# A fused window-attention and expert kernel: first loads as half rows on one queue, mask products on GpSimd only, and a new instruction order

## The chip, the cores and the metric

The kernel runs on one core of a Trainium2 chip. The core has a matrix engine (TensorE), a vector engine (VectorE, DVE in the profile), an activation engine (ScalarE, ACT), a general engine (GpSimd, POOL) and a queue engine (SyncE, SP) that here only issues transfers. The engines run side by side and wait for each other on semaphores. Matmul results go to PSUM, which here is four tiles of two banks. The metric is the time of one execution on the device in microseconds; lower is better. The median of three runs decides.

## The reference

The input is q, k and v of shape (8 batches, 8 heads, 576 tokens, 64). A sliding-window attention comes first, and its output, heads side by side, is the input x of a mixture of four attention experts:

```python
scores = scale * np.matmul(q, k.transpose(0, 1, 3, 2))
mask = np.abs(pos[:, None] - pos[None, :]) <= 32
attn = softmax(np.where(mask, scores, -1e9))          # over keys
x = (attn @ v).transpose(0, 2, 1, 3).reshape(8, 576, 512)

logits = x @ w_gate                                   # 4 experts, the best 2 are kept
w = softmax(the two largest logits)
for e in range(4):
    a = softmax(causal(scale * (x @ wq[e]) @ (x @ wk[e]).T))
    out += (e is chosen) * w[e] * (a @ (x @ wv[e]) @ wo[e])
```

Everything is float32 outside. Inside, the window attention and the gate are in float32, the experts in bfloat16.

## The kernel before

The program is a straight list of steps, written out by hand as text in `ORDER` (895 steps). A loop at the end of the kernel calls one small function for each word. Each engine executes its own instructions in the order of that list, so a step that waits holds up all later steps of the same engine. The letters of a word name the function; the digits name batch, head group (heads 0 to 3 or 4 to 7), half of the tokens, pair of heads or part; after the `@` come the PSUM banks, and the engine of the step where there is a choice (a for ScalarE, v for VectorE, g for GpSimd). The steps of one batch b are:

- `lq`, `lk`, `lv`: load q, k (one head group: 576 KB) and v (128 tokens of all heads: 256 KB). `load` makes each of them wait until the last matmul that stands before it in the list is done. They are all issued by SyncE.
- `tq`, `tk` (`turn`): q and k come with 18 consecutive tokens in one partition, a head in 32 partitions. VectorE transposes 32 x 32 blocks into `QKT`, one transpose for each half of the head dimension.
- `sc`: scores of one head group and one half of the queries, 80 matmuls on 32 rows each, only on the key blocks that the window touches.
- `ex`: ScalarE takes the exponential into `A` (`AT`); there are three such buffers, one for each head group in flight.
- `mk`: `A` times the 0/1 window mask `MASKP`, two heads and 288 queries at once (128 x 576 float32). Eight of these for each batch, 64 in all. `s_mask` builds `MASKP`.
- `vc`: shifted copies of v inside SBUF.
- `av`, `un`: attention times v for 128 tokens, with the row sum as a 65th column, and the division on VectorE into `XN`. The parts T = 0 and 1 (queries 32 to 287) need the four masked products of the first half, T = 2 and 3 (288 to 543) those of the second half, and T = 4 (the first and the last 32 queries) all eight.
- `xt`, `xf`, `xb`: transposes of x on TensorE (with `ident`, built by `s_ident`), copy to `XTF` in float32, cast to `XTB` in bfloat16.
- `ga`, `gt`, `ge`, `gm`, `gu`: the gate. `pp`, `pe`, `pv`, `ve`: expert projections and their evictions. `ps`, `xe`, `se`: expert scores, exponential, causal mask on GpSimd. `po`, `oe`, `ox`, `py`, `ye`, `st`: the values, weights, output projection and store.
- `wl`, `cw`: weight loads and casts. `s_...`: constants and fills. `s_wm`: 30 matmuls on zeros at the start. `s_pada` fills part of the three `ATE` buffers.

Batch 0 starts differently. `fq`, `fk` (`first_load`) and `gq`, `gk` (`first_turn`) load and turn its q and k. For head group 0 the tokens come in two parts of consecutive tokens (tokens 0 to 287 and 288 to 575 for q, 0 to 319 and 320 to 575 for k), one transfer for each head: 16 transfers of 64 to 80 KB. The k transfers are issued by SyncE, the q transfers by ScalarE. Head group 1 comes in one transfer of 576 KB each.

All but one of the 64 mask products run on GpSimd; the step `mk0001@v` puts one of batch 0 on VectorE. Around it, the list reads

```
mk0110@g vc01@g lv12 wl0 ex0100@4 ex0101@0 sc100@62 av03@0 vc00@a wl1 ex1001@2 ex1000@6 mk0101@g tq11
mk0001@v av02@4 sc101@62 mk0100@g tk11 un03@0 un02@4 cw0@a ex1010@6 lq20 mk1001 mk1000 mk1010 ex1011@2
av01@0 un01@0 ...
```

All engine instructions pass through one helper, so nearly all have its line, L145, in the profile; they are told apart by the names of the tiles. Loads are L234 (`load`), L366 and L370 (`first_load`).

Of the kernel before, what the change touches and what calls it, by code (L numbers as in the profile page):

```python
# [20 lines left out]
HS = 288  # L21
# [3 lines left out]
    s_ident s_mask s_padv@g s_onev fq01 s_onep fk00 fk01 fq10 gk00 s_warm fq00 gq01 gk01 gq10 fk10 s_wm lv02  # L25
    lk10 sc001@02 lv00 lv01 lq10 gq00 sc000@46 ex0011@2 ex0010@0 gk10 ex0000@4 tk10 lv03 lq11 sc011@02 lv04
    lk11 ex0110@0 sc010@40 mk0011@g ex0111@2 s_pada@g mk0000@g mk0010@g mk0111@g ex0001@6 tq10 s_padx
    mk0110@g vc01@g lv12 wl0 ex0100@4 ex0101@0 sc100@62 av03@0 vc00@a wl1 ex1001@2 ex1000@6 mk0101@g tq11
    mk0001@v av02@4 sc101@62 mk0100@g tk11 un03@0 un02@4 cw0@a ex1010@6 lq20 mk1001 mk1000 mk1010 ex1011@2
    av01@0 un01@0 lk21 av00@4 lk20 un00@4 xt01@2 av04@0 xf01@2a cw1@a xt00@4 un04@0 xf00@4v xb00@v xb01@g  # L30
    xt02@0 sc110@26 xf02@0a xb02@g mk1011 lv11 lv14 ex1100@2 ex1101@6 tq20 sc111@04 ex1111@4 pp001@2
    pe001@2a lv13 mk1101 pp000@4 ex1110@0 pe000@4a lv10 pp011@6 tk20 pe011@6a wl2 pp010@0 ps000@6 ps003@4
    tk21 ga0@2 gt0@2 gm0@2 pe010@0a xe003@4 xe000@6 mk1111 mk1110 mk1100 ge0@2 gu0@2 vc11@g sc201@40
    ex2010@4 lq21 ps002@6 av14@3 xe002@6 ex2011@0 av13@4 lv23 un14@3 ps011@6 ps001@2 un13@4 mk2010 se001
    vc10@g av12@0 cw2@v xe011@6 lv33 xe001@2 lq30 un12@0 sc200@46 ex2001@6 xt12@2 xf12@2a xt11@0 ex2000@4
    tq21 mk2001 ps013@6 xf11@0a xe013@6 av10@2 un10@2 lv20 lv21 av11@4 ps012@6 xb11@g xe012@6 sc211@20
    ex2111@0 ex2110@2 lv22 wl3 un11@4 xt10@4 sc210@06 tq30 xb12@v ps010@2 xf10@4a lk31 ex2100@0 xe010@2
    ex2101@6 xb10@v se003 mk2000 ga1@4 lq31 pp101@0 pp100@6 lv24 lv30 gt1@4 gm1@4 ge1@4 mk2011 gu1@4
    pe101@0v pv10@2 pp110@0 lv32 vc21@a lk30 mk2100 se011 se000 mk2101 ve10@2a cw3@a pv00@4 pe100@6v
    pe110@0a ps100@2 ps102@0 mk2110 mk2111 av24@6 ve00@4a tk31 pv01@7 av23@4 xe100@2 tq31 un24@6 av22@2 lv31  # L40
    xe102@0 pv11@6 vc31@a lk40 ve11@6a ve01@7a un23@4 un22@2 vc20@g se010 av21@0 av20@4 sc311@62 ex3111@2
    mk3111 se013 un21@0 lq41 ps103@0 un20@4 xt21@4 lq40 xe103@0 ex3110@6 po000@2 pp111@6 xf21@4a xb21@g
    vc30@g tk30 oe000@2 pe111@6a po010@4 ps110@6 lv44 lv34 oe010@4 sc300@20 xt22@4 xf22@4v xb22@g xe110@6
    ex3001@0 ex3000@2 xt20@6 xf20@6v xb20@v ps111@4 sc301@20 ox00 xe111@4 tq40 tk40 ex3011@0 ex3010@2 ox01
    lv42 lv40 sc310@64 ps112@0 se103 mk3000 ex3101@4 mk3101 xe112@0 se111 mk3110 pv20@2 lv43 ve20@2a
    ex3100@6 mk3100 mk3010 py01@0 py00@4 ye00@4a ye01@0v mk3001 lk41 pp200@2 pe200@2v tq41 pp201@6 pe201@6a
    sc401@40 lq50 sc400@62 ex4010@4 lq51 ex4011@0 ex4000@6 ex4001@2 ga2@4 ps113@6 mk3011 xe113@6 ps101@0
    tk41 ps200@2 pv21@5 xe101@0 se110 se113 vc41@g mk4001 mk4000 mk4010 av30@6 lv41 gt2@4 xe200@2 un30@6
    av32@0 un32@0 ve21@5a lk51 se101 av31@2 py02@5 un31@2 av33@6 ps201@0 ps203@2 ye02@5a ge2@4 st02 xe203@2
    gm2@4 un33@6 mk4011 av34@5 lk50 xt30@2 xe201@0 lv54 gu2@4 un34@5 xf30@2a po110@6 pp210@0 pe210@0a  # L50
    sc411@24 ex4110@2 ex4111@4 oe110@6 se100 sc410@06 ex4101@6 ex4100@0 tq50 xt31@2 xt32@4 st01 ox11 po100@6
    tk50 xf32@4a xf31@2a pp211@4 xb30@g pe211@4a mk4111 oe100@6 sc500@20 ex5001@0 ex5000@2 sc501@46 ga3@0
    ox10 st00 ex5011@6 ex5010@4 lv50 lv52 ps212@6 tq51 xb32@v ps202@2 ps213@4 mk4100 mk4110 se200 xb31@v
    mk4101 xe213@4 av44@1 mk5001 mk5011 vc40@g mk5000 xe202@2 pp300@4 xe212@6 gt3@0 ge3@0 gm3@0 un44@1
    pe300@4v gu3@0 pp301@2 pe301@2a lv51 lq60 pp311@6 tk51 pe311@6a mk5010 vc50@g ps210@2 xe210@2 ps211@0
    ps300@4 xe300@4 av40@6 av41@2 av43@4 un40@6 xe211@0 ps301@0 xe301@0 ps303@6 se203 se201 se211 se213
    xe303@6 un41@2 lv53 un43@4 av42@2 un42@2 lq61 pv31@4 py12@5 sc511@60 ye12@5a ve31@4a lk60 ex5110@6
    ex5111@0 sc510@42 ex5100@4 ex5101@2 xt40@6 tq60 lv63 xf40@6v se210 mk5111 xt42@0 pp310@4 pe310@4a py10@2
    ye10@2a st10 po210@6 xt41@4 xf41@4a xf42@0a pv30@2 tk60 oe210@6 ve30@2a lv61 xb41@v mk5100 se303 mk5101
    se300 po200@4 ps312@6 xe312@6 oe200@4 ps310@0 xb40@g xe310@0 xb42@g lv62 ox20 st12 lv60 ox21 ga4@2 lq71  # L60
    ps313@6 ps302@4 xe313@6 xe302@4 mk5110 av54@3 sc601@60 ex6011@0 gt4@2 ge4@2 gm4@2 tq61 pp401@4 pe401@4v
    un54@3 gu4@2 ex6010@6 pp400@0 pe400@0a pv40@6 xt52@3 ve40@6a xf52@3v py11@0 ye11@0v ps403@2 xe403@2 lk61
    ps311@4 ps402@6 xe311@4 xe402@6 vc51@g se313 se311 se301 se310 se401 av51@2 un51@2 pv41@0 py22@1 av52@4
    ye22@1v lk70 ve41@0v vc60@a un52@4 av53@6 av50@0 ps401@4 lk71 xe401@4 un53@6 ps400@2 un50@0 xt51@6
    xf51@6a xt50@0 xf50@0a xb50@g xb51@g mk6010 mk6011 lv71 tk61 xb52@v pp411@4 po300@6 xe400@2 pe411@4a
    oe300@6 po310@0 oe310@0 sc610@42 ex6101@2 ex6100@4 pp410@6 pe410@6a ox31 sc600@20 lq70 ex6001@0 sc611@64
    ex6110@6 ex6000@2 ex6111@4 lv73 se400 se403 pp500@0 pp501@6 pe500@0a tk70 pe501@6v tq71 lv64 lv72 py21@2
    mk6101 py20@0 ye21@2a ps500@6 ps501@4 ye20@0a mk6100 vc61@g mk6001 mk6111 mk6000 lv74 ox30 st20 pv50@2
    pp510@0 xe500@6 xe501@4 tq70 pe510@0v ve50@2a pp511@4 mk6110 vc71@g ps410@2 lv70 pe511@4a ps412@0
    ps411@6 xe410@2 av60@4 av61@2 xe412@0 xe411@6 un60@4 pv51@0 py32@1 vc70@g un61@2 st11 ve51@0a ye32@1a  # L70
    av63@4 ps503@2 xe503@2 un63@4 ps502@6 xe502@6 po400@0 ps510@4 oe400@0 xe510@4 ps511@6 xe511@6 av62@2
    sc700@04 ga5@6 ex7000@0 ex7001@4 ps413@0 un62@2 xe413@0 se413 se503 se411 tk71 ps512@2 ps513@4 ox40
    av64@7 xt60@0 xe512@2 xe513@4 xt61@4 gt5@6 ge5@6 xf60@0a un64@7 xt62@7 se410 po410@2 gm5@6 py31@0
    xf61@4a xf62@7v xb60@v oe410@2 ye31@0v mk7000 xb62@g ga6@7 sc711@24 ex7110@2 ex7111@4 xb61@g se510
    pp600@0 gt6@7 ge6@7 pp601@2 pe601@2a pe600@0a gu5@6 gm6@7 gu6@7 pp610@4 pe610@4a sc710@26 se501 mk7110
    mk7111 se513 ex7100@2 se500 ex7101@6 sc701@40 ex7010@4 ex7011@0 pp611@2 pe611@2a py30@4 mk7001 ps600@0
    ps601@2 ye30@4v se511 xe601@2 po500@6 xe600@0 st21 ox41 py40@4 ye40@4a mk7100 mk7101 mk7010 oe500@6 st32
    st22 st31 se600 po510@2 oe510@2 ps613@6 xe613@6 ps611@0 ps612@4 av71@6 ox50 un71@6 st40 ox51 xe611@0
    xe612@4 mk7011 py42@2 av70@0 ye42@2v st42 av73@4 pv61@2 un70@0 ve61@2a av72@6 st30 un73@4 un72@6 ps603@2
    ps602@0 ps610@4 se613 xe603@2 av74@2 se611 xe602@0 xe610@4 xt70@6 py51@0 xt71@4 un74@2 xt72@2 xf70@6a  # L80
    xf71@4a xb70@v xf72@2a xb71@v xb72@g pv60@6 py50@2 ve60@6a se601 se610 ye50@2a pp700@4 py41@6 pe700@4v
    ye41@6v se603 pp711@2 po610@4 pp701@6 ye51@0a pe701@6a pp710@0 pe711@2v pe710@0a po600@2 ps713@0 xe713@0
    se713 oe610@4 st50 oe600@2 ps710@6 xe710@6 ps711@4 xe711@4 st41 ga7@0 ps712@6 xe712@6 gt7@0 ge7@0 gm7@0
    gu7@0 ps700@2 pv70@4 ps703@6 xe700@2 se711 ps701@2 xe703@6 py52@0 pv71@1 ps702@6 xe701@2 se710 ve70@4v
    ve71@1v ye52@0v se700 se703 ox61 po711@4 oe711@4 st51 xe702@6 ox60 py60@2 po701@0 oe701@0 po712@6
    oe712@6 se701 po702@4 pt711@0 st52 oe702@4 ye60@2a ot711@0a py61@2 pt701@0 ye61@2a ot701@0v py62@1
    pt712@4 ot712@4v pt702@5 st60 st61 ot702@5a ye62@1a py70@6 st62 ye70@6a st70 py72@0 ye72@0a st72 py71@4
    ye71@4a st71
"""


class Watched:

    def __init__(self, tc):
# [52 lines left out]
def kernel(  # L149
# [12 lines left out]
    nc = Watched(tc)  # L162
# [195 lines left out]

    FIRST = {"qn": ((0, 9), (9, 18)), "kn": ((0, 10), (10, 18))}

    def first_load(nm, src, q_, g, x):
        t = NAT[nm][g][:, :, :].rearrange("p o d -> p (o d)")
# [16 lines left out]
    def fk(g, x):  # L381
        first_load("kn", k, nc.sync, g, x)
# [329 lines left out]
```

The softmax here doesn't subtract the row's maximum and nothing guards it: scores larger than these inputs give would overflow.

## Time and profile before

| what | before |
|---|---|
| time, median of 3 runs | 245.62 us (244.63 to 248.32) |
| span of the profiled execution | 242.5 us |
| VectorE product A, MASKP | 1 in 7.34 us |
| GpSimd products A, MASKP | 63, mean 1428 ns |
| VectorE transposes of q and k, 128 x 576 | 60, mean 1240 ns |
| transfers | 42.94 MB, mean 177 GB/s |

The span is the time from the first to the last instruction of one profiled execution. The busy time of an engine is an average over the whole span; what an edit is worth is seen only in its own stretch of the timeline. The start of the kernel, in which loads, transposes, scores and masks of the first batches must follow each other, differs from the rest, in which batches overlap. GpSimd's idle time before its mask products, where it waited for ScalarE's exponentials, is 23.0 us in total.

### The profile page before, as it was taken

Reading aid. Unit: us, or ns where it says so; the run is one execution under the profiler, and the core shown is the slowest. Engines: PE = TensorE matmul, PEld = TensorE weight load, DVE = VectorE, ACT = ScalarE, POOL = GpSimd, SP = SyncE. Lnnn points to the kernel's source line nnn. Section 1 sums busy time; section 2 is a strip of 40 time slices with the busy share of each in tenths; the row PEclk is TensorE's granted clock in tenths of the full one; section 3 lists DMA queues with packets and bytes.
Section 4 is the critical chain, followed back from the end, with each engine's and each line's share of the span. In section 5 each row is a group of like instructions: output and inputs, shape, how many; then the busy total and the mean of one; then the engine's idle time right before and its main releaser. Section 6 shows DMA issues by size and latency. Waiting matters only on the chain.

```text
span 242.5 us, 12237 instructions
## 1 busy us (share of the span) xinstructions
PE 213.7 (88%) x5496; PEld 175.1 (72%) x5496; DVE 179.5 (74%) x354; ACT 151.1 (62%) x234; POOL 155.3 (64%) x176
## 2 busy tenths in 40 slices
PE   6579509898999999998989998999998999999990
PEld 5458508777888987897759876788687886977660
DVE  2687994998779979899969696885858745826760
ACT  2036610657779768767576685776888368674972
POOL 8179940887977287998997791239972889230310
PEclk9855956999999999999999999999999999999997
DMA  6999923475899679789365766573766250715646
GB/s 166 287 246 284 220 95 126 140 179 168 218 276 244 176 234 167 243 238 222 118 145 144 233 173 142 190 229 115 170 224 58 71 153 5 208 45 203 114 169 247
DMA packets 64693, 42.94 MB, mean 177 GB/s; under 512 B 54912, under 2 KB 55936, under 8 KB 64640
## 3 DMA queue, kind: packets, MB, share of 16 engines
q1 hardware_dynamic: 64032, 40.91, 63.8%
q10 hardware_dynamic: 608, 1.25, 1.9%
q8 instruction: 43, 0.70, 1.2%
q14 instruction: 10, 0.08, 0.1%
HBM read 30.42 MB, written 9.44 MB: 164 GB/s over the span
## 4 chain that ended last, share of the span: by engine, by line
PE 64%; DVE 16%; DMA 10%; issue 4%; ACT 3%; ACTq 0%; SPq 0%; DVEq 0%
PE PS L145 64%; DMA qn<-in_q_dram 8%; DVE Tkn L145 4%; DVE A L145 3%; DVE Tqn L145 3%; DMA kn<-in_k_dram 2%; ACT ATE L145 2%; DVE XN L145 1%; DVE PS L145 1%; DVE OE L145 1%; DVE XTB L145 1%; DVE QKE L145 1%; DVE XTF L145 1%; DVE VE L145 0%; DVE m L145 0%
## 5 line engine op out<-in xcount | busy, mean ns | idle before, releaser
L145 POOL TENSOR_TENSOR A<-A,MASKP 128x576 f32<-128x576 f32 x63 | 88.5, 1428 | 23.4 <-ACT A L145 23.0
L145 ACT ACTIVATE ATE<-PS 128x1024 bf16<-128x1024 f32 (+1 forms) x64 | 50.9, 839 | 11.4 <-PE PS L145 11.1
L145 ACT ACTIVATE A<-PS 128x576 f32<-128x576 f32 x64 | 38.5, 652 | 28.8 <-PE PS L145 21.2
L145 PE MATMUL PS<-Tqn,Tkn 32*64 32x128 f32 (+2 forms) x2560 | 47.3, 281 | 5.4 <-DVE Tkn L145 2.8
L145 PE MATMUL PS<-V,A 128*64 128x65 f32 (+1 forms) x1280 | 41.2, 227 | 10.2 <-DVE XN L145 7.7
L145 PEld LDWEIGHTS PS<-Tqn,Tkn 32*64 32x64 f32 x2560 | 42.1, 143 | 10.7 <-DVE Tkn L145 3.2
L145 PEld LDWEIGHTS PS<-V,A 128*64 128x64 f32 (+1 forms) x1280 | 37.6, 136 | 13.8 <-DVE XN L145 7.9
L145 DVE STREAM_TRANSPOSE Tkn<-kn 128x576 f32<-128x576 f32 (+2 forms) x34 | 37.0, 1175 | 10.4 <-DMA kn<-in_k_dram 8.2
L145 POOL TENSOR_SCALAR_AFFINE_SELECT ATE<-ATE 128x512 bf16<-128x512 bf16 (+1 forms) x48 | 24.2, 520 | 24.4 <-ACT ATE L145 21.8
L145 DVE STREAM_TRANSPOSE Tqn<-qn 128x576 f32<-128x576 f32 (+1 forms) x34 | 37.2, 1175 | 3.5 <-DMA qn<-in_q_dram 3.5
L145 POOL CAST XTB<-XTF 128x128 bf16<-128x128 f32 (+1 forms) x18 | 11.7, 670 | 24.2 <-ACT XTF L145 22.8
L145 DVE TENSOR_TENSOR XN<-PS,RC 128x512 f32<-128x512 f32 (+1 forms) x40 | 25.5, 638 | 1.4
L145 POOL COPY V<-V 64x1024 f32<-64x1024 f32 (+1 forms) x24 | 23.2, 965 | 2.9 <-DMA V<-in_v_dram 1.1
L145 ACT COPY XTF<-PS 128x1024 f32<-128x1024 f32 (+1 forms) x23 | 14.9, 696 | 14.0 <-PE PS L145 14.0
L145 ACT CAST QKE<-PS 128x576 bf16<-128x576 f32 x23 | 14.5, 641 | 13.3 <-PE PS L145 13.3
L145 PE MATMUL PS<-ident,XN 128*128 128x128 f32 x144 | 19.2, 280 | 2.0 <-DVE XN L145 1.2
L145 PE MATMUL PS<-WO,OTT 128*128 128x512 bf16 (+1 forms) x96 | 19.2, 345 | 0.4 <-DVE G L145 0.4
L145 PE MATMUL PS<-XTB,WQ 128*128 128x288 bf16 x128 | 18.5, 286 | 0.3 <-issue 0.3
L145 PE MATMUL PS<-XTB,WK 128*128 128x288 bf16 x128 | 18.2, 286 | 0.7 <-DVE XTB L145 0.7
L145 PE MATMUL PS<-WV,XTB 128*128 128x256 bf16 (+1 forms) x192 | 18.6, 255 | 0.0
L145 PEld LDWEIGHTS PS<-ident,XN 128*128 128x128 f32 x144 | 15.9, 142 | 3.6 <-DVE XN L145 1.8
L145 PEld LDWEIGHTS <-ATE 128*128 128x128 bf16 x480 | 16.5, 97 | 2.6 <-issue 1.3
(67 smaller groups left out, 251.4 us busy)
## 6 DMA issues: line engine op xcount, KB each, us to landing
kn<-in_k_dram SPq DMA_DIRECT2D x15, 576.0 KB, 5.0
V<-in_v_dram SPq DMA_DIRECT2D x32, 256.0 KB, 3.8
out_dram<-Y SPq DMA_DIRECT2D x16, 512.0 KB, 3.3
qn<-in_q_dram SPq DMA_DIRECT2D x14, 576.0 KB, 5.1
V<-in_v_dram SPq DMA_DIRECT2D x8, 128.0 KB, 4.0
out_dram<-YS SPq DMA_DIRECT2D x15, 64.0 KB, 2.8
qn<-in_q_dram ACTq DMA_DIRECT2D x8, 72.0 KB, 4.0
qn<-in_q_dram ACTq DMA_DIRECT2D x1, 576.0 KB, 5.3
```

The lines of the kernel that those rows point to most:

```text
L145: return lambda *a, **k: self._w.note(self._e, f(*a, **k))
```

## The change

There are three edits.

1. The first q and k. Head group 0 of batch 0 is now cut in halves of the 18-token rows: in each partition the first nine tokens, then the other nine. One half of one tensor is one transfer of 128 partitions x 576 elements (288 KB) instead of four. All first loads are issued by SyncE. `first_turn` writes each half with a gap, nine tokens out of each 18. The purpose is fewer issues, none of them in ScalarE's stream.
2. No `mk` step asks for VectorE any more (the function itself is unchanged): all 64 products are on GpSimd.
3. The list is arranged anew by an automatic search (annealing) whose costs for the set-up steps at the start were taken from measurements. The set of steps is the same. The order, the PSUM banks and some engines of copies change: the cast of wq (`cw0`) moves from ScalarE to VectorE, `s_mask` and `s_ident` move from the front to behind the first scores, and the scores of batch 0 are taken in another sequence.

```diff
 ORDER = """
-    s_ident s_mask s_padv@g s_onev fq01 s_onep fk00 fk01 fq10 gk00 s_warm fq00 gq01 gk01 gq10 fk10 s_wm lv02
-    lk10 sc001@02 lv00 lv01 lq10 gq00 sc000@46 ex0011@2 ex0010@0 gk10 ex0000@4 tk10 lv03 lq11 sc011@02 lv04
...
+    s_warm fq00 s_onep s_padx gq00 fk00 gk00 fk01 fq01 gq01 gk01 fk10 lq10 fq10 s_wm lv03 sc000@02 lv02
+    sc001@46 gk10 gq10 lv04 ex0011@6 lk10 ex0001@2 lv01 sc011@26 ex0110@2 lv00 ex0010@4 ex0000@0 lq11
+    ex0111@6 s_padv@g sc010@24 lq20 tq10 s_onev tk10 lk11 sc101@60 vc01@a ex0100@2 ex0101@4 vc00@a s_mask
+    mk0011 mk0001 mk0110 mk0010 mk0111 tq11 av02@4 un02@4 mk0100 mk0000 mk0101 lk21 av03@2 un03@2 ex1010@6
+    ex1011@0 wl0 av04@0 un04@0 s_ident av01@4 un01@4 av00@2 lk20 sc100@06 un00@2 ex1001@6 ex1000@0 tk11 wl1
+    xt02@2 xt00@4 xf02@2a s_pada@g xt01@6 sc111@20 mk1011 xb02@g xf00@4a lv11 xf01@6a lv13 ex1110@2 ex1111@0
+    cw0@v sc110@46 xb00@g ex1101@6 xb01@g pp000@0 lv12 pp010@6 lv14 cw1@a pe000@0a ex1100@4 lv10 mk1001
+    mk1111 mk1010 pp011@2 pp001@4 tk20 tq20 tk21 pe001@4v wl2 ga0@0 mk1000 mk1110 mk1100 mk1101 pe011@2a
...
-    FIRST = {"qn": ((0, 9), (9, 18)), "kn": ((0, 10), (10, 18))}
-
-    def first_load(nm, src, q_, g, x):
+    def first_load(nm, src, g, x):
         t = NAT[nm][g][:, :, :].rearrange("p o d -> p (o d)")
-        if g == 1:
-            q_.dma_start(t, src[0, 4:8].rearrange("h (p o) d -> (h p) (o d)", o=18))
-            return
-        o0, o1 = FIRST[nm][x]
-        for h in range(4):
-            q_.dma_start(t[32 * h:32 * h + 32, 64 * o0:64 * o1],
-                         src[0, h, 32 * o0:32 * o1].rearrange("(p o) d -> p (o d)", p=32))
+        s = src[0, 4 * g:4 * g + 4].rearrange("h (p o) d -> (h p) (o d)", o=18)
+        c = slice(HS * 2 * x, HS * 2 * (x + 1)) if g == 0 else slice(0, HS * 4)
+        nc.sync.dma_start(t[:, c], s[:, c])
 
     def first_turn(nm, g, x):
         if g == 1:
             return turn(nm, 0, 1)
-        o0, o1 = FIRST[nm][x]
         for dh in range(2):
-            nc.vector.transpose(QKT[nm][g][:, dh, 32 * o0:32 * o1].rearrange("q (p o) -> q o p", p=32),
-                                NAT[nm][g][:, o0:o1, 32 * dh:32 * dh + 32])
+            nc.vector.transpose(QKT[nm][g][:, dh, :].rearrange("q (p o) -> q o p", o=18)[:, 9 * x:9 * x + 9, :],
+                                NAT[nm][g][:, 9 * x:9 * x + 9, 32 * dh:32 * dh + 32])
 
     def fk(g, x):
-        first_load("kn", k, nc.sync, g, x)
+        first_load("kn", k, g, x)
 
     def fq(g, x):
-        first_load("qn", q, nc.scalar, g, x)
+        first_load("qn", q, g, x)
...
```

## The prediction

> **What bounds the kernel now.** I read the busy line and the slices of the page first, then the chain of waits, then the timeline of the first 47 us engine by engine, then the waits of TensorE after 47 us.
>
> ```profile
> PE 213.7 (88%) x5496; PEld 175.1 (72%) x5496; DVE 179.5 (74%) x354; ACT 151.1 (62%) x234; POOL 155.3 (64%) x176
> PE   6579509898999999998989998999998999999990
> PEclk9855956999999999999999999999999999999997
> ```
>
> One slice is 6.06 us. TensorE is the bound and is dense from slice 8 on; its gaps and its low clock all lie in the first seven slices. TensorE's timeline there (start, length, what):
>
> ```profile
> 2.07 5.44 PE L145 MATMUL PS<-WZ 128*128 128x224 bf16 x30 [2.07 <-DVE PS L145]
> 7.44 0.34 PE L145 MATMUL PS<-Tqn,Tkn 32*64 32x64 f32 x8
> 10.57 2.26 PE L145 MATMUL PS<-Tqn,Tkn 32*64 32x128 f32 x72 [2.79 <-DVE Tkn L145]
> 14.59 4.97 PE L145 MATMUL PS<-Tqn,Tkn 32*64 32x96 f32 x164 [1.75 <-DVE Tqn L145]
> ...
> 36.82 3.73 PE L145 MATMUL PS<-V,A 128*64 128x65 f32 x64 [7.72 <-DVE XN L145]
> ```
>
> The largest hole, 29.1 to 36.8 us, is put down to VectorE's XN. The chain of waits says what VectorE was doing, and the timeline shows GpSimd beside it:
>
> ```profile
> 24.33 1.01 issue
> 25.34 0.97 DVE Tqn L145
> 26.32 0.11 issue
> 26.42 7.34 DVE A L145
> 33.76 2.25 DVE Tkn L145 x2
> ```
>
> ```profile
> 26.29 6.85 POOL L145 TENSOR_TENSOR A<-A,MASKP 128x576 f32<-128x576 f32 x5
> 26.42 7.34 DVE L145 TENSOR_TENSOR A<-A,MASKP 128x576 f32<-128x576 f32 x1
> 33.69 2.32 DVE L145 STREAM_TRANSPOSE Tkn<-kn 128x576 f32<-128x576 f32 x2
> ```
>
> That is step mk0001@v, the one mask product on VectorE. It lasts 7.34 us and ends 0.62 us after GpSimd's fifth product (26.29 + 6.85 = 33.14). The transposes of tk11 and the normalisation un03 stand behind it; TensorE waits for un03 to free its PSUM bank.
>
> From 47 us on TensorE hardly waits:
>
> ```profile
> PE PS L145 <- issue: 1.4, 3, 0.8
> PE PS L145 <- DVE XN L145: 1.2, 1, 1.2
> PE PS L145 <- ACT A L145: 1.1, 1, 1.1
> PE PS L145 <- DVE G L145: 1.1, 2, 0.7
> ```
>
> Adding the shorter ones gives 6.9 us in 190 us. Then come 5.8 us after the last matmul (236.7 to 242.5) for eviction and store.
>
> **What the Trainium skill says.** The page "SBUF — State Buffer", section "SBUF: two separate sides", calls the port pair that VectorE and GpSimd share an exclusive lock: a VectorE operation with two SBUF inputs against a GpSimd operation that reads SBUF fully blocks. The trace agrees, and is worse than one instruction's wait: five products passed. A one-input VectorE cast got in between two GpSimd instructions (XTB at 44.80 us: 1.86 us against 0.68 free). "TensorE: Matmul & The Clock Gate", Part 1, says that the clock halves after an idle window of about 3.4 us. Here it was 1.00 from 8 to 10 us, 0.73 from 10 to 11 and 0.50 until 24, after TensorE went idle at 7.8; again 0.50 from 32 to 40 after the hole. "Trainium Kernel Development and Optimization", Key Constraints, says that all issuing queues share the same 16 DMA engines and only issue time is saved by using several. The trace agrees: with two queues the DMA share was 0.88 to 1.02 from 2 to 5 and 6 to 10 us. So moving q from ScalarE's queue to SyncE's loses no bandwidth.
>
> **The change, part by part.**
>
> *First loads.* Removed: 16 issues of 64 to 80 KB on two queues. ScalarE's last three q issues ran only from 5.39 to 9.55 us, so the second half of q was turned at 13.83. Added: four issues of 288 KB on SyncE, at some 0.4 us each (before, 0.31 to 0.44). They are out by 2.6 us and no longer the limit. I take the bytes from before's one-microsecond windows (31, 279, 235, 205, 241, 335, 277, 278 GB/s from 1 us on): 295 KB are through at 2.95 us, 590 at 4.2, 885 at 5.55, 1180 at 6.55. Before, the first 608 KB were through at about 4.3 and VectorE was released at 5.50, so I add 1.2 us: the halves land at 4.2, 5.4, 6.8 and 7.8. Halves of 18-token rows hold alternate groups of nine tokens, so no score can start before all four are turned; before, half a score could. Four pairs of half transposes at 1.2 us: the last two run from 7.8 to 10.2. sc000 starts at 10.2 (before 14.6, its partner sc001 finishing at 12.8). If completion takes 0.2 or 2.2 us instead, 9.2 or 11.2.
>
> *Group 1 of batch 0.* Its k and q are now behind on the same queue, with lq10 between: 1770, 2360 and 2950 KB, through at about 8.6, 10.6 and 12.7. gk10 runs 10.2 to 12.4, gq10 13.9 to 16.2 (two transposes of 1.2 us). sc011 starts at 16.2; before, 17.05. Here TensorE has 2 to 3 us of idle. I assume the clock falls again, as before at 10.5, and price a score group at 2.3 us (1.4 at full clock).
>
> *All masks on GpSimd.* Removed: 7.34 us of VectorE and the hole. Added: one product of 1.43 us. Mask building (3.8 us) moves to after s_padv but still ends near 7 us, before the first exponential: hidden by the load wait. The identity (0.6 us) and s_pada (4.0 us) move behind the eight products. Walking: sc011 ends 18.5; ex0110 19.2, ex0010 19.8; sc010 19.8 to 22.1; sc101 to 24.4 (tk10 done near 21). GpSimd takes mk0011 and mk0001 from 14, then mk0110 at 19.2 and five more without a gap at 1.4: the fifth ends 23.4, the eighth 27.6. av02 and av03 fit from 24.4 to 26.6; av04 waits for the eighth, 27.6; av01 and av00 end at 30.5 (1.1 us each), sc100 31.9, the three transposes 34.4. GpSimd meanwhile does identity, s_pada and mk1011 until 33.6, then casts xb02, xb00 and xb01: the last ends near 36.5 after ScalarE's xf01.
>
> *cw0 from ScalarE to VectorE.* Two casts of 0.35 us; each can wait behind one GpSimd instruction of up to 1.4 us (as the 1.86 us cast did), so 0.7 to 3.5 us. wq is asked for after av04 (28.3) and landed in 5.6 us before: 34, plus casts 35 to 37.5. Behind them stand tk20 and tq20, for scores much later. So the projection pp000 starts at about 37.0.
>
> *Checkpoint.* Before its first projection TensorE does the same list of groups in both versions: eight scores, five av, three xt. Before, the first projection starts at 46.81; now at 37.0: 9.8 us saved.
>
> *The rest of the list.* Same steps in another order. Counted over the list, VectorE gets two more VE evictions, one more QKE and two more second-half XTF copies, and loses three XTF copies: under 3 us net, on an engine with 60 us free. GpSimd loses a V copy and gains about as much cast. Just after the checkpoint seven masks of batch 1 remain, 10 us from 37, needed by av13 at 44 (fifth ends 44) and av14 at 47 (last ends 47): just in time. I cost this part at nothing, hidden behind TensorE's 190 us of matmul, though a microsecond or two either way is likely.
>
> Sum: 245.62 - 9.8 = 235.8 us.
>
> **Rivals.**
>
> 1. *Clock stays full.* Each of five early score groups costs 1.4 instead of 2.3, of which about 2 us are on the path (the rest hides in load waits). For: TensorE's idle at 7.5 to 10.2 is shorter than the 3.4 us of the page. Against: before, 2.7 us were enough. With a somewhat denser middle: 245.6 - 11.8 - 0.8 = 233.
> 2. *GpSimd takes the place of VectorE's wait.* The eight products followed by identity, s_pada and seven masks leave it without slack from 19 to 47 us; the just-in-time points above each slip by one or two products, and cw0 waits in full. 3 to 5 us given back: 240. For: in the walk above the fifth and the eighth product each come within a microsecond or so of TensorE's need. Against: in the page's waits TensorE's matmuls never wait for GpSimd's A, only once for its V (1.3 us).
> 3. *The new order loses later.* The 6.9 us of waits after 47 us become 17 or more, since the loads, PSUM banks and GpSimd have 10 us less head start. Then nothing is gained or it is slower: 247. Against: GpSimd is 64% and VectorE 74% busy, and DMA's share in slices 10 to 40 lies mostly between 0.5 and 0.8.
>
> **How the numbers follow.** Chances: forecast 0.60, rival 1 0.16, rival 2 0.16, rival 3 0.08. The likeliest gives 235.8. The range runs from a little under rival 1 (231) past rival 2 (243), and takes in the 1 us of landing time and the 2.8 us of cw0; it leaves out rival 3 and the ends. The 2% bounds are 240.7 and 250.5. Faster: forecast, rival 1 and over half of rival 2, 0.86. Same: the rest of rival 2 and most of rival 3, 0.11. Slower: 0.03.
>
> **What would show it.** In the profile after: no VectorE product on A, and no VectorE instruction over 3 us; the first score matmul at 10.2 (9 to 11.5) with four groups of half transposes just ahead; sc011 near 16, released by VectorE's Tqn; the first XTB projection at 37 (34 to 40); TensorE's waits after that near 7 us in total. I am wrong if the first projection comes after 41, if GpSimd's A heads TensorE's waits, or if waits after the checkpoint pass 12 us.

## The result, and the profile after

The changed kernel takes 235.58 us (median of 4 runs, 233.60 to 237.80), the kernel before in the same comparison 246.13 us (244.63 to 248.32). The ratio is 0.9512 with a 95% interval of 0.9419 to 0.9605: faster by 4 to 6%. (The ratio compares only executions within 1.5% of the fastest of their kernel; the medians alone give 0.957.) The profiled executions span 242.5 us before and 231.9 us after.

The page of the kernel after, the same three lines as of before (busy time, busy tenths of TensorE in 40 slices, granted clock in tenths):

```profile
PE 210.1 (91%) x5496; PEld 170.7 (74%) x5496; DVE 177.5 (77%) x362; ACT 149.4 (64%) x228; POOL 156.5 (67%) x174
PE   6668789999999899789899999999999999999990
PEclk9985999999999999999999999999999999999996
```

The weak slices are still at the front, but those at 5 and at 0 are gone, and there the clock is below 0.8 in one slice instead of four. TensorE's timeline of the kernel after says where (start, length, what, number, and in brackets the idle time before it and what ended it):

```profile
8.25 2.78 PE L144 MATMUL PS<-Tqn,Tkn 32*64 32x96 f32 x160 [1.48 <-DVE Tkn L144]
12.51 0.48 PE L144 MATMUL PS<-Tqn,Tkn 32*64 32x64 f32 x16 [1.48 <-DVE Tqn L144]
13.50 1.15 PE L144 MATMUL PS<-Tqn,Tkn 32*64 32x64 f32 x64 [0.51 <-DVE Tqn L144]
...
20.90 2.51 PE L144 MATMUL PS<-V,A 128*64 128x65 f32 x48
24.75 3.30 PE L144 MATMUL PS<-V,A 128*64 128x65 f32 x112 [1.34 <-issue]
...
34.90 1.51 PE L144 MATMUL PS<-XTB,WQ 128*128 128x288 bf16 x11 [0.33 <-ACT A L144]
```

The hole of 7.7 us is gone. All five av groups run from 20.90 to 28.05, broken only by 1.34 us that no other engine explains. The first projection starts at 34.90 instead of 46.81. That splits the difference of the two spans:

| stretch | before | after | difference |
|---|---|---|---|
| start to first projection | 46.81 | 34.90 | -11.9 |
| first projection to the end of the last matmul (236.70; 225.62) | 189.9 | 190.7 | +0.8 |
| end of the last matmul to the end of the span | 5.8 | 6.3 | +0.5 |
| span | 242.5 | 231.9 | -10.6 |

So all of the gain arises before the first projection, and 1.3 us more pass after it than before. VectorE's and GpSimd's timelines of the kernel after, in that head:

```profile
3.64 1.26 DVE L144 STREAM_TRANSPOSE Tqn<-qn 128x288 f32<-128x288 f32 x2 [0.92 <-DMA qn<-in_q_dram]
6.40 1.26 DVE L144 STREAM_TRANSPOSE Tqn<-qn 128x288 f32<-128x288 f32 x2 [0.42 <-DMA qn<-in_q_dram]
...
31.12 0.78 DVE L144 CAST WQ<-Y 128x512 bf16<-128x512 f32 x2
```

```profile
11.87 2.80 POOL L144 TENSOR_TENSOR A<-A,MASKP 128x576 f32<-128x576 f32 x2 [5.97 <-ACT A L144]
15.38 8.30 POOL L144 TENSOR_TENSOR A<-A,MASKP 128x576 f32<-128x576 f32 x6 [0.71 <-ACT A L144]
...
33.83 9.71 POOL L144 TENSOR_TENSOR A<-A,MASKP 128x576 f32<-128x576 f32 x7
```

GpSimd does the eight products of batch 0 by 23.68, VectorE has none, and the cast `cw0` takes 0.39 us for each half, with no wait for GpSimd. From 40 us on, the whole list of TensorE's waits in the kernel after is:

```profile
PE PS L144 <- issue: 4.5, 6, 1.9
PE PS L144 <- DVE Y L144: 0.9, 1, 0.9
PE PS L144 <- ACT QKE L144: 0.3, 1, 0.3
```

That is 5.7 us. From the start of the first projection on it is 6.1 us, against 6.2 us in the kernel before (the 6.9 us of the prediction take in 0.65 us that end with that start). What is new is that most of it is put down to "issue", a wait that no other engine ends.

### The profile page after: what moved, and what is told of

The parts are those of the page before. It is cut to its first block, busy times and chain, and to the rows that moved or that the text cites. A ratio compares the mean times of both kernels' runs of the same rounds, so it can differ in the third digit from the quotient of the medians.

```text
span 231.9 us, 12219 instructions
## 1 busy us (share of the span) xinstructions
PE 210.1 (91%) x5496; PEld 170.7 (74%) x5496; DVE 177.5 (77%) x362; ACT 149.4 (64%) x228; POOL 156.5 (67%) x174
## 4 chain that ended last, share of the span: by engine, by line
PE 75%; issue 5%; DMA 5%; ACT 5%; DVE 5%; SPq 1%; ACTq 0%; DVEq 0%
PE PS L144 75%; DMA qn<-in_q_dram 3%; DMA V<-in_v_dram 2%; ACT A L144 2%; ACT V L144 2%; DVE XTB L144 1%; SPq L364 1%; DVE XTF L144 1%; ACT QKE L144 1%; DVE Tqn L144 1%; DVE PS L144 0%; DVE Y L144 0%; ACT Y L144 0%; ACT WO L144 0%; DVE OE L144 0%
## 5 line engine op out<-in xcount | busy, mean ns | idle before, releaser
L144 POOL TENSOR_TENSOR A<-A,MASKP 128x576 f32<-128x576 f32 x64 | 89.7, 1424 | 29.1 <-ACT A L144 29.1
L144 ACT ACTIVATE A<-PS 128x576 f32<-128x576 f32 x64 | 37.9, 652 | 31.4 <-PE PS L144 31.3
L144 PE MATMUL PS<-Tqn,Tkn 32*64 32x128 f32 (+2 forms) x2560 | 45.0, 268 | 7.8 <-DVE Tqn L144 2.0
L144 PEld LDWEIGHTS PS<-Tqn,Tkn 32*64 32x64 f32 x2560 | 39.4, 135 | 13.7 <-issue 4.2
L144 DVE STREAM_TRANSPOSE Tkn<-kn 128x576 f32<-128x576 f32 (+1 forms) x34 | 36.9, 1178 | 2.2 <-DMA kn<-in_k_dram 2.2
L144 POOL TENSOR_SCALAR_AFFINE_SELECT ATE<-ATE 128x512 bf16<-128x512 bf16 (+1 forms) x48 | 25.4, 545 | 18.6 <-ACT ATE L144 17.7
L144 POOL COPY V<-V 64x1024 f32<-64x1024 f32 (+1 forms) x22 | 21.1, 961 | 1.3
L144 POOL CAST XTB<-XTF 128x1024 bf16<-128x1024 f32 (+1 forms) x17 | 12.6, 758 | 11.9 <-DVE XTF L144 8.9
L144 PE MATMUL PS<-WV,XTB 128*128 128x256 bf16 (+1 forms) x192 | 18.5, 255 | 0.0
L144 ACT CAST QKE<-PS 128x576 bf16<-128x576 f32 x22 | 13.7, 641 | 7.4 <-PE PS L144 7.4
L144 PEld LDWEIGHTS <-ATE 128*128 128x128 bf16 x480 | 16.2, 97 | 2.2 <-issue 0.5
L144 PE MATMUL PS<-VE,ATE 128*128 128x65 bf16 x480 | 17.0, 193 | 0.4 <-issue 0.4
```

The costliest lines, as they stand in the source:

```text
L144: return lambda *a, **k: self._w.note(self._e, f(*a, **k))
```

## The experiments

The questions were: what each of the three edits is worth (E1 to E4), why the first loads arrive so early (E5, E6), what the "issue" waits are (E8), and whether a product on VectorE is always shut out by GpSimd, as the prediction took it (E7, E9 to E12). "Head" is the start of the first projection in the profiled execution, "rest" the span less the head.

| kernel | median, us | ratio to before (95%) | head | rest |
|---|---|---|---|---|
| before | 246.13 | | 46.81 | 195.7 |
| E1 mask only | 240.95 | 0.9757 (0.9683 to 0.9832) | | |
| E2 loads only | 242.58 | | 44.59 | 198.0 |
| E3 mask and loads | 236.97 | 0.9595 (0.9517 to 0.9673) | 38.04 | 199.5 |
| E4 all but the loads | 238.67 | 0.9683 (0.9619 to 0.9748) | 39.38 | 197.6 |
| E5 two queues | 235.90 | 0.9585 (0.9504 to 0.9667) | 37.02 | 196.2 |
| E6 narrow transfers | 238.56 | 0.9714 (0.9650 to 0.9777) | 41.21 | 196.9 |
| E7 product back, behind tk20 | 235.73 | 0.9579 (0.9498 to 0.9659) | 35.19 | 196.9 |
| E9 product back, behind tq20 | 237.19 | | 38.47 | 197.7 |
| E11 product later | 240.69 (one run) | | 40.91 | 198.0 |
| E12 other product | 246.13 (one run) | | 46.93 | 197.5 |
| after | 235.58 | 0.9512 (0.9419 to 0.9605) | 34.90 | 197.0 |

The rest is 195.7 to 199.5 us in every one of them, in either order of the list, so most of what an edit brings shows in the head. The kernel before has the shortest rest: 0.5 to 3.8 us may be paid back later, which single profiles do not resolve. Heads of nearly equal kernels (after, E5, E7) still lie 2.1 us apart from one execution to another, so single heads are good to about 2 us.

**E1: the mask edit alone.** The kernel before with

```diff
-    mk0001@v av02@4 sc101@62 mk0100@g ...
+    mk0001@g av02@4 sc101@62 mk0100@g ...
```

> The kernel before with one word changed: the mask product mk0001 on GpSimd instead of VectorE; first loads and order as before. Theory (the one VectorE product, held behind GpSimd's run, makes TensorE's hole at 29 to 37 us): no VectorE instruction over 3 us, GpSimd's run one product longer (to about 34.5 us), av01 starts near 30.5 instead of 36.8, the first projection near 40 instead of 46.8; time 6 to 8 us less, 238 to 240. Rival (the hole is set by the loads and scores in front, the product only fills it): 0 to 2 us less, above 244.

The time is 240.95 us; three of the four executions lie between 239.21 and 241.15. (The fourth took 680 us, with TensorE busy for 671.7 us against 213.7 before. It is the one whose profile was kept, so E1 has no head in the table.) Before took 245.83 us on the same chip: one word of the list brings some 5 us, 6 us by the ratio (4 to 8 by its interval), a little under the 6 to 8 expected.

**E2: the new first loads alone.** The kernel before with the new `first_load` and `first_turn`; in the list only `fq00` and `gq00` move forward:

```diff
-    s_ident s_mask s_padv@g s_onev fq01 s_onep fk00 fk01 fq10 gk00 s_warm fq00 gq01 gk01 gq10 fk10 s_wm lv02
+    s_ident s_mask s_padv@g s_onev fq01 s_onep fk00 fk01 fq00 fq10 gk00 s_warm gq01 gk01 gq00 gq10 fk10 s_wm lv02
-    lk10 sc001@02 lv00 lv01 lq10 gq00 sc000@46 ...
+    lk10 sc001@02 lv00 lv01 lq10 sc000@46 ...
```

> The kernel before with the new first loads and half-row transposes alone, all on SyncE's queue (the second half of q is therefore called for with the others at the front); mk0001 stays on VectorE. Theory: the first scores start at 8 to 10 us instead of 10.6 and 14.6, but the VectorE product is still caught behind GpSimd's run, so part of it is lost again; time 2 to 4 us less, 242 to 244. Rival (the early start carries through to the end): 6 us less or more.

242.58 us against 245.83: about 3 us less by the medians, on a spread that does not resolve it (one execution took 235.80 us, the other three 241.94 to 244.40). The scores start at 8.36, but VectorE's product is caught as before. E2's timelines of GpSimd, VectorE and TensorE:

```profile
23.50 6.87 POOL L145 TENSOR_TENSOR A<-A,MASKP 128x576 f32<-128x576 f32 x5
24.66 6.32 DVE L145 TENSOR_TENSOR A<-A,MASKP 128x576 f32<-128x576 f32 x1
...
34.03 3.73 PE L145 MATMUL PS<-V,A 128*64 128x65 f32 x64 [6.10 <-DVE XN L145]
```

GpSimd's five products end at 30.37, VectorE's one at 30.98, 0.61 us later. TensorE then has a hole of 6.10 us. Data that come earlier are in good part used up in front of the same wait: the head is only 2.2 us shorter.

**E3: both edits, the old order.** E1 and E2 together.

> The kernel before with both edits, mask product and first loads, but the rest of its order. Theory (the two parts add up to nearly all of the gain and the new order for the rest is worth nothing): 9 to 11 us less, 235 to 237, within 2 us of the changed kernel. Rival (the new order does the work): 5 us less or under, over 240.

236.97 us, 8.9 us less than before: the two parts add up (5 to 6 and 3). E3 differs from E2 by the one word `mk0001@g` alone, and this pair has profiles: the products are one run of six on GpSimd, and the attention group before which TensorE waited 6.10 us in E2 starts without a wait in E3, behind the scores that end at 28.36:

```profile
28.29 1.15 PE L145 MATMUL PS<-V,A 128*64 128x65 f32 x31
```

The head falls from 44.59 to 38.04 and the median by 5.6 us. What the new order adds is small and not resolved: from E3 to the kernel after the medians differ by 1.4 us, from E1 to E4, the same step with the old loads, by 2.3 us, and in both pairs the intervals of the ratios overlap. The heads of E3 and after differ by 3.1 us, but the one profile is of an execution of 239.34 us and the other of one of 233.60 us.

**E4: the new order and the mask edit, the old loads.** The changed kernel with `FIRST`, `first_load` and `first_turn` of before, k on SyncE and q on ScalarE:

```diff
     def fq(g, x):
-        first_load("qn", q, g, x)
+        first_load("qn", q, nc.scalar, g, x)
...
```

> The changed kernel with the old first loads (16 transfers of 64 to 80 KB, q from ScalarE's queue) and the old split in consecutive tokens; order and masks as changed. Theory (the new loads bring the halves 2 to 4 us earlier, since one queue of 128-partition transfers moves 330 to 400 GB/s in the first 10 us against 205 to 335 before): 2 to 5 us slower than the changed kernel, 237 to 241. Rival (the loads do not matter in the new order): within 1 us of it, 235.

238.67 us: without the new loads 3 us of the gain are missing. With the old parts the first half of the tokens comes first, so one score group starts at 7.47, but the second only at 12.38, after TensorE has waited 3.23 us for VectorE's Tqn; the head is 39.38.

**E5: two queues.** The changed kernel with all first q loads issued by ScalarE, and `s_warm` behind them (the remark in the code is added here).

```diff
-        nc.sync.dma_start(t[:, c], s[:, c])
+        (q_ or nc.sync).dma_start(t[:, c], s[:, c])      # fq: q_ = nc.scalar
```

> The changed kernel with its q first loads (two of 288 KB, one of 576 KB) issued from ScalarE's queue instead of SyncE's; shapes as changed. Theory (the rate in the first 10 us is set by the shape of the transfers, 128 partitions each, not by the number of queues): 330 to 400 GB/s from 3 to 10 us as with one queue, the first score within 1 us of 8.25, time within 2 us of the changed kernel. Rival (two queues disturb each other): 200 to 300 GB/s, first score at 10 or later, 2 us slower.

**E6: narrow transfers.** The changed kernel with each half cut by head: 16 transfers of 32 partitions (72 KB) instead of four of 128 (288 KB), all on SyncE.

```diff
-        nc.sync.dma_start(t[:, c], s[:, c])
+        for h in ((0, 1, 2, 3) if g == 0 else (None,)):
+            r = slice(0, 128) if h is None else slice(32 * h, 32 * h + 32)
+            nc.sync.dma_start(t[r, c], s[r, c])
```

> The changed kernel with each half of the first q and k cut in four transfers of 32 partitions (16 transfers of 72 KB), all on SyncE. Theory (narrow transfers are slower, by their issue at 0.4 to 0.45 us each[...]): the rate from 2 to 8 us falls to 150 to 250 GB/s, the first score starts at 10 to 12 us instead of 8.25, time 1.5 to 4 us more. Rival (only bytes count): first score before 9 us, time unchanged within 1 us.

The view of windows gives the DMA rate from 2 to 10 us (window, its length, granted clock, DMA share, GB/s). First the kernel after, then E6:

```profile
2.00:10.00 8.00, 1.00 0.98 366
```

```profile
2.00:10.00 8.00, 1.00 0.59 156
```

E5 has 375 GB/s and 235.90 us, the same as one queue. E6 has 156 GB/s; its first score starts at 11.69 after a wait of 4.12 us, its head is 41.21 and its time 238.56 us, as with the old loads (E4). So the gain of the first edit is the wide transfer with few issues, not the queue. SyncE's own timeline in E6 says which of the two counts there:

```profile
0.80 1.80 SPq L366 DMA_DIRECT2D qn<-in_q_dram  x4
...
6.36 1.81 SPq L366 DMA_DIRECT2D qn<-in_q_dram  x4
```

The 16 issues follow each other from 0.80 to 8.17 us, one each 0.46 us. 72 KB in 0.46 us are 160 GB/s, as much as was moved, and the DMA engines are counted as busy for 0.59 of the time only. So in E6 the number of issues on one queue sets the rate. In the kernel before, with two queues, it isn't the whole reason: there the engines are counted as 0.95 busy from 2 to 10 us, at 270 GB/s. What narrow transfers cost apart from their issues was not tried.

**E7: one product back on VectorE.** The changed kernel with one product of batch 1 on VectorE, while GpSimd has a row of them:

```diff
-    mk1111 mk1010 pp011@2 pp001@4 tk20 tq20 tk21 pe001@4v wl2 ga0@0 mk1000 mk1110 ...
+    mk1111 mk1010 pp011@2 pp001@4 tk20 mk1000@v tq20 tk21 pe001@4v wl2 ga0@0 mk1110 ...
```

> The changed kernel with one mask product of batch 1 (mk1000) put on VectorE, right behind tk20, while GpSimd has seven products in a row. Theory (VectorE is shut out for the whole of GpSimd's run, not for one instruction): the product lasts 5 to 7.5 us and ends within 0.7 us of the end of GpSimd's run near 42; the turns, eviction and gate behind it come 5 us later, time 2 to 6 us more. Rival (it waits for one GpSimd instruction, 1.4 us, like the casts): at most 2.2 us long, time within 1 us.

E7's timelines of GpSimd and VectorE there:

```profile
34.55 8.82 POOL L144 TENSOR_TENSOR A<-A,MASKP 128x576 f32<-128x576 f32 x6
34.79 1.80 DVE L144 TENSOR_TENSOR A<-A,MASKP 128x576 f32<-128x576 f32 x1
```

My theory fell. VectorE's product waited for one GpSimd product and got in; the time is that of the changed kernel (235.73 us). Being asked for during a row of GpSimd products is not enough to be shut out for the whole row.

**E8: what "issue" is.** A kernel of the start of the changed kernel and then 48 score groups back to back, first with no loads beside them and then with one load after each group; softmax, attention and experts are left out, and zeros are stored.

> A measuring kernel that leaves the whole computation out: after the first q and k of batch 0 are turned, the same score group (80 weight loads and 80 matmuls) 48 times with nothing to wait for, the first 24 with no transfers running, the last 24 with one load of 576 KB called for behind each; the output is filled with zeros. Question: what are TensorE's waits put down to issue, which in the changed kernel end 1.2 to 1.6 us after a 16 KB instruction fetch. Theory A (256 instructions are used up in about 2.2 us of such groups, faster than a fetch is turned round whatever else runs): waits of 0.3 to 2 us in both stretches, a group taking 1.5 to 2.5 us on average. Theory B (fetches are only late behind other transfers): none in the first stretch (1.37 us per group), waits in the second. Theory C (not the fetch): none in either, 66 us for all.

TensorE's timeline of E8, three blocks of the quiet part and one from the part with loads:

```profile
18.72 2.05 PE L82 MATMUL PS<-Tqn,Tkn 32*64 32x96 f32 x128 [1.94 <-issue]
22.18 2.13 PE L82 MATMUL PS<-Tqn,Tkn 32*64 32x128 f32 x128 [1.40 <-issue]
25.63 2.05 PE L82 MATMUL PS<-Tqn,Tkn 32*64 32x64 f32 x128 [1.32 <-issue]
...
118.13 2.13 PE L82 MATMUL PS<-Tqn,Tkn 32*64 32x128 f32 x128 [2.94 <-issue]
```

With nothing else to wait for, TensorE stops after every 128 matmuls. With their weight loads these are 256 instructions. In the kernel after, the page counts these instruction transfers (packets, MB, share):

```profile
q8 instruction: 43, 0.70, 1.3%
```

5496 matmuls and 5496 weight loads are 10992 instructions: there is about one packet of 16 KB for each 256 of them. In E8 it is one between each stall and the next. In the trace's transfer records of E8, all 28 stalls end 1.19 to 1.54 us after the end of such a packet. In the kernel after:

| stall of TensorE | packet, start to end | resumed after its end |
|---|---|---|
| 17.99 to 18.70 (put down to ACT V) | 16.20 to 17.25 | 1.45 |
| 23.41 to 24.75 | 22.46 to 23.35 | 1.40 |
| 32.26 to 32.68 | 30.24 to 31.17 | 1.50 |
| 36.41 to 36.86 | 34.57 to 35.49 | 1.36 |
| 73.06 to 73.42 | 70.79 to 72.12 | 1.30 |
| 77.67 to 78.52 | 76.03 to 77.29 | 1.23 |
| 92.35 to 93.27 | 90.88 to 91.91 | 1.36 |
| 97.34 to 99.29 | 96.70 to 97.72 | 1.57 |

All of these also stand at one place of TensorE's stream: with its semaphore and drain instructions counted, 193 or 194 instructions into a block of 256. So do the 28 of E8 and the three "issue" waits of the kernel before after 47 us. The seven that the profile puts down to "issue" are 6.3 of its 6.7 us: there TensorE waited for its instructions. The Trainium skill, "Runtime: NRT & Kernel Launch", section "Instruction fetch mechanics", says that crossing a 16 KiB block of 256 instructions costs a step that is mostly hidden. For these short matmuls it is not: a block takes 3.45 to 3.73 us in the quiet part, of which some 2.05 are matmuls, and up to 5.1 us beside loads. Theory A held, but for stalls longer than 2 us beside loads.

**E9: the product in another row.** The changed kernel with a product on VectorE in the longest run of products that were all ready:

```diff
-    mk1111 mk1010 pp011@2 pp001@4 tk20 tq20 tk21 pe001@4v wl2 ga0@0 mk1000 mk1110 mk1100 mk1101 pe011@2a
+    mk1111 mk1010 pp011@2 pp001@4 tk20 tq20 mk1101@v tk21 pe001@4v wl2 ga0@0 mk1000 mk1110 mk1100 pe011@2a
```

> The changed kernel with another product of batch 1 (mk1101) on VectorE, behind tq20, at about 38 us, where every product that GpSimd still has in its run (mk1000, mk1110, mk1100) had its exponential ready before VectorE asks. In the run before it, VectorE's product got in behind the first of six GpSimd products (1.80 us); the product that stood next there had its exponential ready only at about 35.0, after VectorE had asked at 34.8. Theory (GpSimd passes the ports on without a gap as long as its next product is ready in time, so VectorE is shut out to the end of such a run): the product lasts 3.5 to 5 us and ends about 0.6 us after GpSimd's last product near 42; tk21, the QKE eviction and the gate come 3 to 4 us later, and the time is 0 to 3 us more. Rival (the wait is always one instruction, and the 7.34 us of the kernel before have another cause): at most 2.1 us long, time within 1 us of the changed kernel.

VectorE's product, asked for in a run of five on GpSimd (38.40 to 45.85), took 1.17 us at 40.65: in after one product again, though GpSimd's run has no idle time. This theory fell too. The time was 237.19 us (234.67 to 239.17), before 245.13 (238.08 to 248.57), too wide for a ratio.

**E10: the products by themselves.** Only products: 24 times a row of five or six on GpSimd and one on VectorE, with no, one, two or three transposes ahead of it and with the tiles of the kernel before, of E7 and of E9. All else is left out.

> A measuring kernel that leaves the whole computation out (arrays of zeros, output filled with zeros) and runs 24 trials: GpSimd does a row of mask products with no waits between them (five as they stood in the kernel before around mk0001; five and six as in the two runs that put a product of batch 1 on VectorE), and VectorE asks for one mask product 0, 1, 2 or 3 transposes (about 1.2 us each) after the row starts; each set twice. Theory A (which buffers and halves the row holds decides: the row of the kernel before shuts VectorE out): in the first four trials of each half the product lasts 2.5 to 7 us with GpSimd's products at 1.36 us distance; in the others at most 2.1 us. Theory B (the lock goes to VectorE at the first change of instruction, and the 7.34 us came from waits between GpSimd's instructions and other engines): at most 2.1 us in all trials. Theory C (without waits between them GpSimd's products pass the lock on among themselves): all rows shut VectorE out to their end, 2 to 8 us long.

VectorE's timeline of E10, a trial that VectorE starts and one that it does not:

```profile
13.46 0.69 DVE L82 TENSOR_TENSOR A<-A,MASKP 128x576 f32<-128x576 f32 x1
22.89 1.48 DVE L82 TENSOR_TENSOR A<-A,MASKP 128x576 f32<-128x576 f32 x1
```

0.69 us when it comes first, 1.48 to 1.64 us in the other 18 trials: it waits for the GpSimd product that runs, and goes next, as theory B had it. The row of the kernel before is among them, so which tiles are multiplied is not the cause by itself.

**E11: the product asked for later.** The kernel before with its one VectorE product moved behind `tk11`:

```diff
-    mk0001@v av02@4 sc101@62 mk0100@g tk11 un03@0 ...
+    av02@4 sc101@62 mk0100@g tk11 mk0001@v un03@0 ...
```

> The kernel before with mk0001 still on VectorE but behind the transposes of tk11 instead of ahead of them, so that VectorE asks about 2.3 us later, in the second or third of GpSimd's five products. What is open: VectorE was shut out for five products here, but got in behind one in the changed kernel and in the quiet row. Theory A (this row of GpSimd, in its place in the kernel, lets nobody in): the product again ends 0.6 us after the last GpSimd product, 4 to 5.5 us long. Theory B (it was the moment of asking): at most 2.2 us long, and the hole of TensorE at 29 to 37 us shrinks by 3 us or more, time 241 to 244.

E11's timelines of GpSimd and VectorE:

```profile
25.82 5.54 POOL L145 TENSOR_TENSOR A<-A,MASKP 128x576 f32<-128x576 f32 x4
29.50 2.48 DVE L145 TENSOR_TENSOR A<-A,MASKP 128x576 f32<-128x576 f32 x1
```

GpSimd's run ends at 31.36, as it waits for ScalarE, and VectorE's product 0.62 us later; it asked in the third product, the fourth passed it, and it was shut out to the end of the run again; but the run was nearly over. Theory A was right on the end of the wait, theory B on the smaller hole. TensorE's hole fell from 7.7 to 2.32 us and the time from 244.28 to 240.69 us, one run each.

**E12: another product in the same place.** The kernel before with `mk0001` on GpSimd and `mk0100` on VectorE:

```diff
-    mk0001@v av02@4 sc101@62 mk0100@g tk11 ...
+    mk0001@g av02@4 sc101@62 mk0100@v tk11 ...
```

> The kernel before with mk0100 on VectorE in the same place instead of mk0001, which goes to GpSimd. Theory A (the row and its place decide): 6 to 7.5 us long, ending 0.6 us after GpSimd's run, time as before, 244 to 247. Theory C (the product on this very part of the buffer decides): at most 2.2 us long, TensorE's hole shrinks by 4 us or more, time 239 to 242.

E12's timelines of GpSimd and VectorE:

```profile
27.16 5.51 POOL L145 TENSOR_TENSOR A<-A,MASKP 128x576 f32<-128x576 f32 x4
27.87 5.41 DVE L145 TENSOR_TENSOR A<-A,MASKP 128x576 f32<-128x576 f32 x1
```

The product took 5.41 us and ended 0.61 us after GpSimd's run of four. TensorE's hole was 3.98 us, the head 46.93, the time 246.13 us in one run: the shut-out follows the place, as theory A had it, and not the product.

So in this place of the list, four kernels (before, E2, E11, E12) show VectorE shut out to the end of GpSimd's run, for 2.48 to 7.34 us, always ending 0.61 to 0.62 us after it, while in another place of the changed kernel (E7, E9) and by themselves (E10) one product passes at most. The moment of asking does not decide by itself: it lies 0.13, 0.71, 0.92 and 1.16 us after the start of a GpSimd product in the first four, and 0.24 and 0.87 us in E7 and E9. What hands the ports on from one GpSimd product to the next there stays open, and so does whether it happens each time: one execution of the kernel before took 238.08 us (in the comparison of E9; all others 243.69 to 248.57) and one of E2 235.80, each some 7 us under its median, about the size of the hole. Neither has a profile.

## Why the prediction was right, step by step

The forecast was 235.8 us with the likeliest case, and the measurement is 235.58. The mechanism held: the gain is made before the first projection, and what is paid for it later, 1.3 us between two profiles, is not resolved. That the number came so close is in part luck. The sum hides two misses that nearly cancel, 2.1 us too little gain in the head and 1.3 us too little loss in the rest, and the median of before was 0.5 us higher in the comparison than in the forecast.

- *First loads, the landing times.* This term was mis-sized. The forecast used before's rates of 205 to 335 GB/s; with wide transfers it was 366 from 2 to 10 us. E4, with before's transfers in the new order, has 254 GB/s. VectorE was released by the q halves, the first and the fourth to be issued, at 3.64 and 6.40 instead of 4.2 and 7.8. The first score started at 8.25 instead of 10.2: 1.85 us after the last release instead of 2.4, as it needed only three of the last four half transposes. I had carried the rate of 16 narrow transfers over to four wide ones; E6 shows that cutting them up is what costs the rate. That one queue loses nothing held (E5).
- *Group 1 and the clock.* sc011 was expected to start at 16.2 and end at 18.5, and started at 12.51 and ended at 14.65. Most of this, 2.8 us, is the loads again: both waits ahead of it were ended by VectorE's Tqn, whose transposes could start at 11.10 instead of 13.9. The clock, assumed to fall at about 10, stayed at 1.00 until 16 us, and the first two score groups took 2.78 us together instead of 4.6; but that time went into the wait for Tqn. The clock did fall then, to a mean of 0.57 from 16 to 24 us, and a score group cost the half-clock price (80 matmuls in 2.27 us at 18.70). Rival 1 was right on the clock of the first groups only.
- *All masks on GpSimd.* Right in kind: without the one product on VectorE the hole goes (E2 against E3). E1 brings 5 to 6 us, less than the hole of 7.7 us. The eighth product ended at 23.68 instead of 27.6, as much earlier as the scores were. E11 and E12 add that the wait came with the place of the step.
- *"Worse than one instruction's wait: five products passed."* True of that trace, but I had taken it for what always happens, and E7, E9 and E10 show that it is not. The Trainium skill, "SBUF — State Buffer", section "SBUF: two separate sides", speaks of a block for one whole instruction, and these three agree with it; before, E2, E11 and E12 exceed it. The forecast didn't need the general form, only that this one wait goes.
- *cw0.* 0.7 to 3.5 us allowed, 0.78 measured: its lower end. No product ran on GpSimd at that time, and it did not hold up the first projection. That came at 34.90 rather than 37.0: TensorE's own score groups ran until 34.57, and then it waited 0.33 us for ScalarE's exponential.
- *The rest at nothing.* +0.8 us between first projection and last matmul, +0.5 in the tail. The waits are no longer than before (6.1 against 6.2 us), and the runs of one kernel spread over 4 us, so this is not resolved. Of the 6.1 us, 4.5 stand in the table of E8 as instruction fetch, which the forecast did not have at all.
- *The rivals.* GpSimd did not take the place of the wait: no wait of TensorE in the kernel after is put down to GpSimd. The new order did not lose later either: the rest is 197.0 us, inside the range of the table. It gained little as well: the same kernels with the old order are 1.4 us (E3) and 2.3 us (E1 against E4) behind, neither resolved.

In the head the earlier start of 3.9 us at the end of sc011 shrank to 2.1 us at the first projection. The stalls of 0.71, 1.34 and 0.41 us in the table of E8 stand between the two, 2.5 us in all. Before, TensorE ran much of this stretch at half clock: 164 score matmuls in 4.97 us are 3.9 us for 128, longer than the 3.45 us that a block takes in E8. That a faster clock so turns in part into waiting for instructions is worked out from these rows, not tried by itself.

## What to carry to other kernels

Find the stretch in which the bound engine is not dense and ask which instruction of another engine stood in front of what it waited for: here one word of a list of 895 was worth half of the gain, and earlier data alone met the same wait. Don't carry a transfer rate from one shape to another, and count the issues: four transfers of 288 KB moved data more than twice as fast as 16 of 72 KB, each of which took 0.46 us to issue. Where TensorE's waits are put down to "issue", compare them with its instruction transfers before looking for a semaphore.

## What the runs showed of the hardware that was not expected

- TensorE's instruction stream has a rate of its own: 256 instructions in 3.45 us at best (E8), with stalls of 1.3 to 1.9 us a block in the quiet part and up to 2.94 us beside loads, always 193 instructions into a block of 256. 32-row score matmuls at full clock run into it.
- A VectorE product against a row of GpSimd products waits for one of them (at most 1.80 us in all in E7, E9, E10) or for the rest of the run (up to 7.34 us). The four runs of the second kind are the kernel before and its variants, at one place of the list; what decides is open.
- The wide first transfers reached 366 GB/s over 8 us from one queue and 375 from two, against 254 (E4, 16 issues on two queues) and 156 GB/s (E6, 16 issues of 0.46 us on one queue).
